# Halving three times on VectorE in the last tiles of a one-query attention

## The chip, the cores and the metric

The kernel runs on one core of one Trainium2 chip. The metric is device time in microseconds (us). A core that runs alone cannot be compared with its neighbours, so a run's state is judged from the other runs of the same kernel; all profiled runs here count as fast. Medians are given with their ranges. Ratios are computed as the mean time of one kernel's fast runs over that of the other's of the same rounds, so they are not quite the ratio of the quoted medians.

## The reference

```python
B, H, Sq, Skv, Dh = 8, 32, 1, 4096, 128          # bf16 q, k, v
scores = jnp.einsum('bhqd,bhkd->bhqk', q, k) * q.shape[-1] ** -0.5
attn = softmax(scores, axis=-1)
return jnp.einsum('bhqk,bhkd->bhqd', attn, v)
```

There are 256 heads with one query each. Every byte of K and V (537 MB together) is read once and used for one query, so the arithmetic per byte is small.

## The kernel before

Eight heads form a tile; there are 32 tiles (0 to 31), `C` = 256 rows per partition and `D` = 128. K and V tiles of 8.39 MB share three buffers. VectorE multiplies K by q in place and folds the products of each row in halves; TensorE finishes the fold by adding slices through an identity matrix into PSUM; VectorE reduces what is left to scores.

```python
LT = NT - 3                                   # tile 29
def width_of(t, lo):
    return D // 8 if lo == C // 2 and 0 < t < NT - 3 else D // 2

def product(t, lo, hi):
    part = kt[:, lo:hi, :]
    nc.vector.tensor_tensor(out=part, in0=part, in1=qb..., op=ALU.mult)
    n = D
    while n > width_of(t, lo):
        n //= 2
        nc.vector.tensor_tensor(out=part[:, :, 0:n], in0=part[:, :, 0:n],
                                in1=part[:, :, n : 2 * n], op=ALU.add)

def sum_over_d(t, lo, hi):
    ds = BANK // (hi - lo)                    # BANK = 512
    n = width_of(t, lo) // ds
    for s in range(n):
        nc.tensor.matmul(ps[:], lhsT=ident[:], rhs=kt[:, lo:hi, s * ds : (s + 1) * ds], ...)
# ... cut: scores, weights, value matmuls
# the last V tile is loaded in pieces, so that the end is short:
("v", NT - 1): [C // 2, C // 4, C // 8, C // 16, LAST // 2, LAST // 4, LAST // 4]
```

Tiles 1 to 29 are worked on in halves; the others in quarters. From tile 1 to tile 28 the second half is folded from 128 to 16 values; all other parts only from 128 to 64. A V tile is issued when the sums of the K tile whose buffer it takes are done; a K tile when the value matmuls of an older V tile are. For V tile 31 it is the value matmuls of tile 29.

Of the kernel before, what the change touches and what calls it, by code (L numbers as in the profile page):

```python
# [25 lines left out]
def kernel(  # L26
# [8 lines left out]
    B, H, Sq, D = q.shape  # L35
# [5 lines left out]
    C = S // PH  # L41
    NT = NH // G
# [85 lines left out]
    w_last = consts.tile([P, LAST, RG], BF16, name="w_last")  # L128
    nc.gpsimd.memset(w_last[:], 0.0)

    loads = {}
    loops = []

# [17 lines left out]
    def load(kind, t):  # L151
        src = k_t if kind == "k" else v_t
        buf = kv_pool.tile([P, C, D], BF16, name=f"{kind}t", tag="kv")
        c0 = 0
        for n in cuts.get((kind, t), [C]):
            dma = nc.sync.dma_start(buf[:, c0 : c0 + n, :], src[t, :, c0 : c0 + n, :])  # L156
            behind_loop(dma)
            c0 += n
            if kind == "k" and t == 0 and c0 == n:
                nc.sync.dma_start(q_all[:], q_n)  # L160
        assert c0 == C
        loads[kind, t] = buf
# [3 lines left out]
    def q_prep(t):  # L166
        x, p0 = divmod(t * G, P)
        qh = ps_q.tile([G, D], F32, name="qh", tag="qp")
        nc.tensor.matmul(  # L169
            qh[:], lhsT=ident[:, p0 : p0 + G], rhs=q_all[:, x, :], start=True, stop=True  # L170
        )
        qg = q_pool.tile([G, D], BF16, name="qg", tag="qg")
        nc.scalar.activation(out=qg[:], in_=qh[:], func=ACT.Copy)  # L173
        qp = ps_q.tile([P, D], F32, name="qp", tag="qp")
        nc.tensor.matmul(qp[:], lhsT=heads[:].rearrange("g h x -> g (h x)"), rhs=qg[:], start=True, stop=True)  # L175
        qb = q_pool.tile([P, 1, D], BF16, name="qb", tag="qb")
        nc.scalar.activation(out=qb[:, 0, :], in_=qp[:], func=ACT.Copy)  # L177
        qbs[t] = qb

    def width_of(t, lo):  # L180


        return D // 8 if lo == C // 2 and 0 < t < NT - 3 else D // 2

    def product(t, lo, hi):
        kt = loads["k", t]
        qb = qbs[t]
        part = kt[:, lo:hi, :]
        nc.vector.tensor_tensor(  # L189
            out=part, in0=part, in1=qb[:].to_broadcast([P, hi - lo, D]), op=ALU.mult  # L190
# [4 lines that stand above are left out]
            nc.vector.tensor_tensor(  # L195
                out=part[:, :, 0:n], in0=part[:, :, 0:n], in1=part[:, :, n : 2 * n], op=ALU.add
            )
# [3 lines left out]
    def sum_over_d(t, lo, hi):  # L201
        kt = loads["k", t]
        ps = ps_s.tile([P, BANK], F32, name="ps", tag="ps")
        ds = BANK // (hi - lo)
        n = width_of(t, lo) // ds
        for s in range(n):
            nc.tensor.matmul(  # L207
                ps[:], lhsT=ident[:], rhs=kt[:, lo:hi, s * ds : (s + 1) * ds],
                start=(s == 0), stop=(s == n - 1),
            )  # L210
        sums[t, lo] = ps
# [3 lines left out]
    def scores_of(t, lo, hi):  # L215
        if lo == 0:
            scs[t] = sc_pool.tile([P, C], F32, name="sc", tag="sc")
        ps = sums.pop((t, lo))[:].rearrange("p (c s) -> p c s", c=hi - lo)
        made = nc.vector.tensor_reduce(  # L219
            out=scs[t][:, lo:hi], in_=ps, axis=AX.X, op=ALU.add  # L220
        )
        if hi == C:
            behind_loop(made)
# [74 lines left out]
                one(i, start=False, stop=(i == NV - 1))  # L298
        loops.append(loop)

    LT = NT - 3

    def values_of(t, lo, hi):
        vt = loads["v", t]
        w = ws[t]
        if lo == 0:
            avs[t] = ps_v.tile([P, CB * D], F32, name="av", tag="av")
        end = C if t < NT - 1 else C - LAST


        group = [
            0 if t == NT - 1 and C // 2 <= c0 < C // 2 + 3 * C // 32 else c0 // CB % TG
            for c0 in range(0, end, CB)
        ]
        for c0 in range(lo, hi, CB):
            i = c0 // CB
            j = group[i]
            nc.tensor.matmul(  # L318
                avs[t][j * AG : (j + 1) * AG, :], lhsT=w[:, i, :, :],
                rhs=vt[:, c0 : c0 + CB, :], start=(i < TG), stop=(j not in group[i + 1 :]),  # L320
            )
# [6 lines left out]
    def norm_of(n):  # L328
        zp = ps_z.tile([RG, 1], F32, name="zp", tag="zp")
        esum = esums.pop(n)  # L330
        for r in range(R):
            nc.tensor.matmul(  # L332
                zp[:], lhsT=mine[:, r, :], rhs=esum[:, r : r + 1], start=(r == 0), stop=(r == R - 1)
            )
        zps[n] = zp
# [7 lines left out]
    def copy_of(t):  # L343
        comb = o_pool.tile([P, CB, D], BF16, name="comb", tag="comb")
        av = avs.pop(t)[:].rearrange("p (m d) -> p m d", d=D)
        n = AG if t < LT else P
        nc.scalar.activation(out=comb[0:n, :, :], in_=av[0:n, :, :], func=ACT.Copy)  # L347
        combs[t] = comb

    def result_of(t):  # L350
        n, r = divmod(t, R)
        comb = combs.pop(t)
        if r == 0:
            ops[n] = ps_o.tile([RG, D], F32, name="op", tag="op")
        e = AG if t < LT else P

        def last_rows(lo, hi):
            for i in range(lo, hi):
                nc.tensor.matmul(  # L359
                    ops[n][:], lhsT=w_last[:, i, :], rhs=loads["v", t][:, C - LAST + i, :],  # L360
                    start=False, stop=(i == LAST - 1),
                )

        if t == NT - 1:
            last_rows(0, 3 * LAST // 4)
        for m in range(CB):
            nc.tensor.matmul(  # L367
                ops[n][:], lhsT=pick[0:e, m, r, :], rhs=comb[0:e, m, :],
                start=(r == 0 and m == 0), stop=(r == R - 1 and m == CB - 1 and t < NT - 1),
            )  # L370
        if t == NT - 1:
            last_rows(3 * LAST // 4, LAST)
# [17 lines left out]
    Q, HALF = C // 4, C // 2  # L390
# [3 lines left out]
    with tc.manual_schedule(engines={E.PE, E.DVE, E.Activation, E.SP}):  # L394
        q_prep(0)
        q_prep(1)
        for t in range(NT):
            loop = 0 < t <= LT
            v_last = t >= NT - 2
            n = t // R - 1  # L400
            if not loop:
                if t + 1 < NT:
                    load("k", t + 1)
                load("v", t)
            first = HALF if loop else Q
            product(t, 0, first)
            if not loop:
                sum_over_d(t, 0, first)
            if 0 < t - 1 <= LT:
                if (t - 1) % R == 0:  # L410
                    norm_of(n)
                if t > 1:
                    result_of(t - 2)
            if t + 2 < NT:
                q_prep(t + 2)
            if loop:
                sum_over_d(t, 0, HALF)
                product(t, HALF, C)
                sum_over_d(t, HALF, C)
                scores_of(t, 0, HALF)  # L420
                if t > 2 and t % R == 1:
                    recip_of(n)
                values_loop(t - 1)
                load("k", t + 1)
                load("v", t)
                scores_of(t, HALF, C)
            else:
                product(t, Q, HALF)
                sum_over_d(t, Q, HALF)
                scores_of(t, 0, Q)  # L430
                product(t, HALF, HALF + Q)
                sum_over_d(t, HALF, HALF + Q)
                scores_of(t, Q, HALF)
                if t > 2 and t % R == 1:
                    recip_of(n)
                product(t, HALF + Q, C)
                sum_over_d(t, HALF + Q, C)
                scores_of(t, HALF, HALF + Q)
            if v_last:
                values_of(t - 1, 0, C)  # L440
            if not loop:
                scores_of(t, HALF + Q, C)
            weights_of(t)
            if t > 2 and t % R == 1:
                finish_of(n)
            if t > 0:
                copy_of(t - 1)
                if t > 2 and t % R == 1:
                    store_of(n)
                if not loop:  # L450
                    if t % R == 0:
                        norm_of(n)
                    result_of(t - 1)
        values_of(NT - 1, 0, C // 2)
        norm_of(NQ - 1)
        recip_of(NQ - 1)
        values_of(NT - 1, C // 2, C - LAST)
        copy_of(NT - 1)
        result_of(NT - 1)
        finish_of(NQ - 1)  # L460
        store_of(NQ - 1)
# [30 lines left out]
```

## Time and profile before

| | before |
|---|---|
| median (3 runs) | 1250.9 us (1250.84 to 1250.91) |
| load queue | 536.94 MB, 99.5% of 16 DMA engines' span |
| mean load rate | 430 GB/s |
| VectorE busy | 1010.6 us (81%) |
| TensorE busy | 761.4 us (61%) |

Each digit of the profile's DMA row is a fortieth of the span, and 9 is 90% or more: the row is full. The execution that was profiled took 1251.34 us, 0.4 us more than the median: it is not one of the three runs in the table.

### The profile page before, as it was taken

What the parts mean: (1) busy time and instruction counts of PE and PEld (TensorE: products, weight loads), DVE (VectorE), ACT (ScalarE), POOL (GpSimd) and SP (SyncE); (2) the same over time, 40 slices, a digit from 0 to 9 for tenths busy, and PEclk for the clock granted to TensorE, in tenths of its full rate; (3) what the DMA queues carried; (4) which work ended last, traced back from release to release, by engine and by line L of the source; (5) the groups of instructions that cost most, each with busy time, mean ns of one, the idle gap of its engine ahead of it and who ended that gap; (6) DMA issues with size and microseconds to landing.
All of it is one profiled execution on the core that took longest, in us unless ns stands there. A gap on an engine that the chain in (4) does not pass through costs nothing. (4 is left out here: it accounts for less than half of the span.)

```text
span 1249.5 us, 10534 instructions
## 1 busy us (share of the span) xinstructions
PE 761.4 (61%) x3004; PEld 284.3 (23%) x3004; DVE 1010.6 (81%) x379; ACT 166.1 (13%) x433; POOL 4.5 (0%) x24
## 2 busy tenths in 40 slices
PE   3356457554586555766557665577655676556855
PEld 1122122221222212222122222122221222212312
DVE  7877987778977789777797777987779877798694
ACT  0111011111011110111101111011110111101111
POOL 1000000000000000000000000000000000000000
PEclk9786798777887777878678777887867877778867
DMA  9999999999999999999999999999999999999998
GB/s 405 436 436 435 436 429 424 426 436 437 436 432 435 435 434 434 435 435 426 431 436 435 426 430 436 435 434 437 433 432 430 433 437 432 433 432 425 429 442 339
DMA packets 11430, 537.30 MB, mean 430 GB/s; under 512 B 1808, under 2 KB 2064, under 8 KB 2320
## 3 DMA queue, kind: packets, MB, share of 16 engines
q1 hardware_dynamic: 11072, 536.94, 99.5%
q8 instruction: 14, 0.23, 0.1%
q10 hardware_dynamic: 336, 0.07, 0.0%
q14 instruction: 8, 0.07, 0.0%
HBM read 536.94 MB, written 0.07 MB: 430 GB/s over the span
## 5 line engine op out<-in xcount | busy, mean ns | idle before, releaser
L189 DVE TENSOR_TENSOR kt<-kt,qb 128x16384 bf16<-128x16384 bf16 (+1 forms) x70 | 556.8, 7955 | 156.8 <-DMA kt<-in_k_dram 150.1
L207 PE MATMUL ps<-kt,ident 128*128 128x512 bf16 x688 | 253.2, 537 | 416.3 <-DVE kt L195 415.9
L290 PE MATMUL av<-vt,w 128*32 x1740 | 425.3, 397 | 4.4
L195 DVE TENSOR_TENSOR kt<-kt 128x4096 bf16<-128x4096 bf16 (+1 forms) x126 | 382.7, 3037 | 4.3
L290 PEld LDWEIGHTS av<-vt,w 128*32 x1740 | 173.3, 100 | 262.1 <-issue 118.9
L207 PEld LDWEIGHTS <-ident 128*128 128x128 bf16 x688 | 80.0, 125 | 583.0 <-DVE kt L195 444.7
L244 ACT ACTIVATE e<-sc,nmax 128x256 bf16<-128x256 f32 x32 | 16.2, 508 | 708.0 <-DVE nmax L238 708.0
L251 ACT ACTIVATE w<-e,mine 128x256 bf16<-128x256 bf16 x256 | 105.6, 495 | 1.1
L219 DVE TENSOR_REDUCE sc<-ps 128x128 f32<-128x512 f32 (+1 forms) x70 | 48.1, 687 | 57.0 <-PE ps L207 57.0
L347 ACT ACTIVATE comb<-av 32x512 bf16<-32x512 f32 (+1 forms) x32 | 18.8, 586 | 327.3 <-PEq L280 320.9
L276 PE MATMUL av<-vt,w 128*32 128x512 bf16 x116 | 47.1, 498 | 14.5 <-issue 13.3
L367 PE MATMUL op<-comb,pick 32*16 32x128 bf16 (+1 forms) x128 | 12.2, 213 | 21.9 <-ACT comb L347 21.9
L276 PEld LDWEIGHTS av<-vt,w 128*32 128x32 bf16 x116 | 6.9, 101 | 54.7 <-issue 54.7
L175 PE MATMUL qp<-qg,heads 8*128 8x128 bf16 x32 | 7.0, 217 | 16.7 <-ACT qg L173 16.7
L367 PEld LDWEIGHTS <-pick 32*16 32x16 bf16 (+1 forms) x128 | 8.7, 83 | 28.9 <-issue 28.5
L231 DVE TENSOR_REDUCE pmax<-sc 128x1 f32<-128x256 f32 x32 | 13.4, 420 | 1.1
L318 PE MATMUL av<-vt,w 128*32 128x512 bf16 x188 | 13.7, 417 | 0.0
L173 ACT ACTIVATE qg<-qh 8x128 bf16<-8x128 f32 x32 | 8.5, 267 | 33.5 <-PE qh L169 33.5
L169 PE MATMUL qh<-q_all,ident 128*8 128x128 bf16 x32 | 7.2, 225 | 8.7 <-DMA q_all<-in_q_dram 8.3
L177 ACT ACTIVATE qb<-qp 128x128 bf16<-128x128 f32 x32 | 8.9, 278 | 9.7 <-PE qp L175 9.7
L339 DVE RECIPROCAL rz<-zp 16x1 f32<-16x1 f32 x16 | 2.3, 147 | 8.1 <-PE zp L332 8.1
L233 DVE TENSOR_SCALAR spread<-same,pmax 128x32 f32<-128x32 f32 x32 | 7.7, 242 | 1.1
(30 smaller groups left out, 45.7 us busy)
## 6 DMA issues: line engine op xcount, KB each, us to landing
kt<-in_k_dram SPq DMA_DIRECT2D x4, 4096.0 KB, 23.8
kt<-in_k_dram SPq DMA_DIRECT2D x4, 2048.0 KB, 12.3
vt<-in_v_dram SPq DMA_DIRECT2D x1, 4096.0 KB, 33.1
vt<-in_v_dram SPq DMA_DIRECT2D x1, 2048.0 KB, 37.6
vt<-in_v_dram SPq DMA_DIRECT2D x1, 1024.0 KB, 39.7
vt<-in_v_dram SPq DMA_DIRECT2D x1, 512.0 KB, 40.5
vt<-in_v_dram SPq DMA_DIRECT2D x31, 26.2
kt<-in_k_dram SPq DMA_DIRECT2D x29, 28.7
```

The costliest lines, as they stand in the source:

```text
L189: nc.vector.tensor_tensor(out=part, in0=part, in1=qb[:].to_broadcast([P, hi - lo, D]), op=ALU.mult)
L195: nc.vector.tensor_tensor(out=part[:, :, 0:n], in0=part[:, :, 0:n], in1=part[:, :, n : 2 * n], op=ALU.add)
L207: nc.tensor.matmul(ps[:], lhsT=ident[:], rhs=kt[:, lo:hi, s * ds : (s + 1) * ds], start=(s == 0), stop=(s == n - 1),)
L219: made = nc.vector.tensor_reduce(out=scs[t][:, lo:hi], in_=ps, axis=AX.X, op=ALU.add)
L231: nc.vector.tensor_reduce(out=pmax[:], in_=sc[:], axis=AX.X, op=ALU.max)
L244: nc.scalar.activation(out=e[:], in_=sc[:], func=ACT.Exp, bias=nmax[:, 0:1], scale=scale, accum_out=esums[t // R][:, t % R : t % R + 1],)
L251: nc.scalar.activation(out=w[:, :, g, :], in_=e_g, func=ACT.Copy, scale=mine[:, 0, g : g + 1])
L276: pe.matmul(av, lhsT=wf[:, i * nw : (i + 1) * nw], rhs=vf[:, i * nv : (i + 1) * nv], **how)
L290: pe.matmul(av, lhsT=wf[:, bass.ds(ow + i * nw, nw)], rhs=vf[:, bass.ds(ov + i * nv, nv)], start=False, stop=False,)
L318: nc.tensor.matmul(avs[t][j * AG : (j + 1) * AG, :], lhsT=w[:, i, :, :], rhs=vt[:, c0 : c0 + CB, :], start=(i < TG), stop=(j not in group[ ...
L347: nc.scalar.activation(out=comb[0:n, :, :], in_=av[0:n, :, :], func=ACT.Copy)
L367: nc.tensor.matmul(ops[n][:], lhsT=pick[0:e, m, r, :], rhs=comb[0:e, m, :], start=(r == 0 and m == 0), stop=(r == R - 1 and m == CB - 1 an ...
```

## The change

The intent: in three places near the end, TensorE needs 16 or 8 identity matmuls to finish a sum, at half clock, while VectorE waits. Folding these parts further on VectorE leaves 4 or 2 matmuls, so that the buffers come free and the weights are ready earlier.

```diff
     def width_of(t, lo):
-        return D // 8 if lo == C // 2 and 0 < t < NT - 3 else D // 2
+        if t == 0:
+            return D // 2
+        return D // 8 if lo == (C // 2 if t <= LT else 3 * C // 4) else D // 2
```

The rest of the diff moves `LT` up and renames `loop` to `halves`. So tile 29's second half and the last quarters of tiles 30 and 31 are now folded to 16 values.

More of the change, by code (lines that the diff above doesn't have):

```diff
@@ L129 @@
     nc.gpsimd.memset(w_last[:], 0.0)
+    LT = NT - 3
     loads = {}
@@ L299, in values_loop @@
         loops.append(loop)
-    LT = NT - 3
     def values_of(t, lo, hi):
@@ L397 @@
         for t in range(NT):
-            loop = 0 < t <= LT
+            halves = 0 < t <= LT
             v_last = t >= NT - 2
             n = t // R - 1
-            if not loop:
+            if not halves:
                 if t + 1 < NT:
@@ L404 @@
                 load("v", t)
-            first = HALF if loop else Q
+            first = HALF if halves else Q
             product(t, 0, first)
-            if not loop:
+            if not halves:
                 sum_over_d(t, 0, first)
@@ L415 @@
                 q_prep(t + 2)
-            if loop:
+            if halves:
                 sum_over_d(t, 0, HALF)
@@ L440 @@
                 values_of(t - 1, 0, C)
-            if not loop:
+            if not halves:
                 scores_of(t, HALF + Q, C)
@@ L449 @@
                     store_of(n)
-                if not loop:
+                if not halves:
                     if t % R == 0:
```

## The prediction

> **What bounds the kernel now.** I read the page first: its busy slices, its queue table, and its costliest groups.
>
> ```profile
> PE 761.4 (61%) x3004; PEld 284.3 (23%) x3004; DVE 1010.6 (81%) x379; ACT 166.1 (13%) x433; POOL 4.5 (0%) x24
> ...
> DMA  9999999999999999999999999999999999999998
> GB/s 405 436 436 435 436 429 424 426 436 437 436 432 435 435 434 434 435 435 426 431 436 435 426 430 436 435 434 437 433 432 430 433 437 432 433 432 425 429 442 339
> ...
> q1 hardware_dynamic: 11072, 536.94, 99.5%
> ...
> L189 DVE TENSOR_TENSOR kt<-kt,qb 128x16384 bf16<-128x16384 bf16 (+1 forms) x70 | 556.8, 7955 | 156.8 <-DMA kt<-in_k_dram 150.1
> L207 PE MATMUL ps<-kt,ident 128*128 128x512 bf16 x688 | 253.2, 537 | 416.3 <-DVE kt L195 415.9
> ```
>
> The DMA row shows no free slice, and the load queue is busy for 99.5% of the span. VectorE (DVE) is busy for 81% and spends 150.1 us waiting for K to land; TensorE (PE) waits 416 us for VectorE. So everything computes faster than data arrives. Each K or V tile is 128 x 256 x 128 bf16 = 8.39 MB, which at the page's mean of 430 GB/s takes 19.5 us; 64 tiles take 1,249 us of a 1,249.5 us span.
>
> A bound that holds on average may still break at the end, where the change sits, so I read the chain of waits that ended last.
>
> ```profile
> 1196.02 3.40 PE ps L207 x8
> 1199.41 3.60 PE av L318 x64
> 1203.01 0.02 issue
> 1203.03 0.33 SPq L156
> ...
> 1204.83 40.66 DMA vt<-in_v_dram
> 1245.48 0.04 issue
> 1245.53 0.83 PE op L359 x12
> 1246.36 0.22 PE op L367 x4
> 1246.58 0.24 PE op L359 x4
> ```
>
> The tempting reading is that the eight matmuls at 1196.02, which the change cuts to two, gate the issue of the last V tile and hence the end. But 40.66 us from issue to landing is twice what a tile needs at 430 GB/s: the transfer stood in a queue. V tile 30 was issued at 1199.45 and tile 31 from 1203.03, and those two alone need 39.0 us (2 x 19.5). Counting back from 1246 they start flowing at about 1207, so the rest of K tile 31 still occupied the queue for some 7 us after 1199.45. The stretches confirm it:
>
> ```profile
> 1180.00:1200.00 20.00, 10.97 (x46) 3.69 (x48) 15.68 (x8) 0.00 (x0) 0.00 (x0) 0.74 0.97 414
> 1200.00:1227.00 27.00, 14.25 (x88) 4.86 (x80) 26.76 (x15) 4.39 (x11) 0.00 (x0) 0.61 1.00 431
> 1227.00:1240.00 13.00, 8.29 (x91) 3.51 (x95) 4.17 (x6) 4.63 (x12) 0.76 (x4) 0.76 0.98 418
> 1240.00:1246.20 6.20, 6.07 (x69) 3.25 (x59) 0.16 (x1) 0.60 (x1) 0.00 (x0) 0.72 0.67 258
> ```
>
> The last three columns are TensorE's clock, the DMA share and GB/s. DMA is full up to 1240 and falls only while the small last pieces of V drain.
>
> **What the Trainium skill says.** "DMA: Bandwidth & Descriptors", section "Where 436 GB/s comes from", derives a ceiling of 435.2 GB/s from the 16 memory ports; the slices here reach 432 to 437, so it agrees and no room is left in the rate. "VectorE: DVE Perf Modes", section "Side-by-side: where the cycles go for N=2048 bf16", counts half a cycle per element in the two-per-cycle mode plus about 158 cycles at 0.96 GHz: 1224 ns for 2048 elements; the trace has 1225. "TensorE: Matmul & The Clock Gate", part 1, says that the array runs at half clock until it has been busy for about 3.4 us (512 columns then start every 427 ns instead of 216) and falls back after an idle window; the trace agrees, with a granted clock of 0.50 or 1.00 and eight matmuls of 512 columns in 3.60 us at 0.50.
>
> **The change part by part.** Halving from 64 to 16 values per row adds two VectorE adds and divides the identity matmuls of that part by four.
>
> Tile 29, second half: it adds one add of 4096 elements (2.29 us in the groups by shape, but 2.21 from start to start because the ends overlap) and one of 2048 (1.23 busy, 1.14 start to start): 3.35 us. It takes 16 matmuls down to 4. The sixteen took 6.47 us here; four took 1.89 us for tile 28, which already has this form. Saved 4.58, net 4.58 - 3.35 = **1.2 us** earlier for this tile's scores, for the issue of V tile 29 (now 1162.25), and for the loop of value matmuls behind it, which takes 16.7 us on tiles 27 and 28 alike.
>
> Tiles 30 and 31, last quarter: one add of 2048 elements (1.14) and one of 1024. No 1024-element add exists in this trace; the steps 4425, 2292, 1225 ns halve their distance each time and give 0.69 us, and the skill's count gives (512 + 158)/0.96 GHz = 0.70, an estimate; some 0.60 start to start. So 1.74 us are added. Eight matmuls become two: two at half clock are estimated at 1.05 us (0.63 for one, as its longest record, plus 0.43). Tile 30's eight took 3.40 and tile 31's 3.60, so 0.6 and 0.8 us are gained.
>
> Sum of the path: 1.2 + 0.6 + 0.8 = **2.6 us** earlier for the weights of tile 31, which ScalarE now finishes at 1238.39 (1235.09 + 3.30). V tile 30's issue moves from 1199.45 to about 1197.6, V tile 31's to about 1201.5. All of this only makes queue entries older: the same bytes still leave at the same rate, and the 40.66 us of the last wait become about 42. VectorE work rises by 3.5 + 2 x 1.9 = 7.4 us to about 1018, inside its idle time. TensorE loses 12 + 6 + 6 = 24 matmuls.
>
> The end then. Here is TensorE's work from the last weights on:
>
> ```profile
> 1239.39 2.96 PE L318 MATMUL av<-vt,w 128*32 128x512 bf16 x29
> 1242.14 0.29 PE L332 MATMUL zp<-esum,mine 128*16 128x1 f32 x4
> 1242.30 3.09 PE L318 MATMUL av<-vt,w 128*32 128x512 bf16 x28
> 1245.53 0.83 PE L359 MATMUL op<-vt,w_last 128*16 128x128 bf16 x12
> 1246.19 0.39 PE L367 MATMUL op<-comb,pick 128*16 128x128 bf16 x4
> 1246.42 0.39 PE L359 MATMUL op<-vt,w_last 128*16 128x128 bf16 x4
> ```
>
> The first half of V tile 31 lands at 1236.2 (issued at 1203.03, 33.1 us to landing), the 2 MB piece at about 1241.1, the 1 MB piece at about 1243.6, the 512 KB piece at about 1244.9 and the last 128 KB at 1246.2 (issued at 1226.5, 19.7 us). Four matmuls of the 28 read the 512 KB piece, so these 28, whose last one ends at 1245.39, are already at the heels of the data. The weights being 2.6 us earlier moves the first 32 value matmuls from 1239.2 to about 1236.5, but the last 28 cannot end before 1245.2, the copy of 0.60 us and the closing matmuls follow as now, and the last 128 KB is needed anyway. I put the gain of the whole change at **0 to 0.3 us**.
>
> **The rivals.** (a) *The chain is taken at its word*: V tile 31 is issued 1.5 us earlier and so ends earlier, for 1249.4. For it: the chain does run through these matmuls. Against: the full DMA row and the 40.66 us. It would hold only if the queue ran dry near 1200. (b) *A colder TensorE at the end*: with the weights earlier, TensorE finishes the first half by 1238 to 1240 and then idles until 1241.1. Today it works without a gap from 1239.2, and the clock is 0.55 in 1241.1 to 1243.7 and 1.00 after. If the gap delays the return of the full clock, the first six of the 28 matmuls, which add into one place one after another, cost 6 x 0.43 = 2.6 us (to 1243.7), and the other 22, four at a time, 0.107 each = 2.4 us (to 1246.1 instead of 1245.0). That is 1.1 us later, up to 1.5 with the closing matmuls: 1252.0 to 1252.4. Against: a stretch two thirds busy may count as busy. I give it one chance in three. (c) *VectorE becomes the bound*: 7.4 us more work where it has nearly no gap (26.76 of 27 us in 1200 to 1227). Against: each add replaces a longer wait for matmuls, and V does not need VectorE; had all 7.4 us come on top, the weights would be ready at 1245.8 and the end some 7 us later, 1258. One chance in fifty.
>
> **Range and chances.** No change two times in three (1250.6 to 1251.1, as the runs agree within 0.1 us), 1 to 1.5 us slower nearly one time in three, a fraction of a microsecond to 1.5 faster otherwise. The weighted middle is 1251.0, range 1250.0 to 1252.4. Two per cent is 25 us; the work that the change touches lies in the last 95 us, all under a full DMA queue, so faster or slower by that has one chance in a hundred each.
>
> **What would show it.** Right: VectorE about 1018 us and x385, TensorE x2980, the last 512-column sums of tiles 30 and 31 x2, V tile 30 issued near 1197.6, the last V wait lengthened to about 42 us, weights of tile 31 near 1235.8, the last V landing within 0.5 us of 1246.2. Wrong: a DMA share visibly below 0.97 between 1180 and 1227, V landing earlier by as much as it was issued earlier, or a last landing moved by over 1 us. Rival (b) shows as a granted clock of 0.50 after 1243.7 with the copy of the last values later than 1246. What could spoil the whole estimate is a load rate that reacts to VectorE's changed timing; nothing in the slices hints at it.

## The result, and the profile after

| | before | after |
|---|---|---|
| median | 1250.9 us (1250.77 to 1251.86, 6 runs) | 1251.45 us (1251.4 to 1251.59, 6 runs) |
| ratio | | 1.0004, 95% interval 0.9991 to 1.0016 |

The change makes no difference worth the name. Yet there is a small pattern. Five of the six runs before lie at 1250.77 to 1250.91, the sixth at 1251.86, and all six after at 1251.4 or more. The computed interval includes 1 all the same. We come back to this half microsecond below.

The page of the changed kernel:

```profile
PE 759.8 (61%) x2980; PEld 282.2 (23%) x2980; DVE 1017.9 (81%) x385; ACT 166.1 (13%) x433; POOL 4.4 (0%) x24
...
DMA  9999999999999999999999999999999999999997
...
q1 hardware_dynamic: 11072, 536.94, 99.5%
```

The work changed exactly as counted (VectorE six instructions and 7.3 us more, TensorE 24 matmuls fewer) and the load queue looks as before. The chain of waits that ended last:

```profile
1194.52 1.24 DVE kt L197
...
1195.78 0.70 DVE kt L197
...
1196.53 1.03 PE ps L209 x2
1197.56 6.03 PE av L318 x47
...
1203.61 0.33 SPq L157
...
1205.41 40.28 DMA vt<-in_v_dram
...
1245.74 0.83 PE op L359 x12
```

The two new adds (1.24 and 0.70 us) and the pair of matmuls in 1.03 us are there. V tile 30 is issued at 1197.60 instead of 1199.45. But the issue of V tile 31 moved from 1203.03 to 1203.61: in this execution it is **later**. The 64 value matmuls of tile 29 before it took 6.07 us instead of 3.64, because TensorE got its full clock late: 1197.5 to 1203.6 shows a mean clock of 0.59 here and 0.87 before. This differs from one execution to the next. In a second trace of the same kernel (run change_again below) the clock was 0.76 there, the 64 matmuls took 5.10 us, and V tile 31 was issued at 1202.59, earlier than before. And 1205.41 + 40.28 is still 1245.7: neither the earlier nor the later issue shows in the landing.

TensorE from the last weights on, and the stretches around it (the third last column is the clock):

```profile
1236.97 1.89 PE L318 MATMUL av<-vt,w 128*32 128x512 bf16 x29
1238.69 0.24 PE L332 MATMUL zp<-esum,mine 128*16 128x1 f32 x4
1241.37 1.89 PE L318 MATMUL av<-vt,w 128*32 128x512 bf16 x16 [2.44 <-DMA vt<-in_v_dram]
1243.84 0.62 PE L318 MATMUL av<-vt,w 128*32 128x512 bf16 x8 [0.58 <-DMA vt<-in_v_dram]
1245.09 0.40 PE L318 MATMUL av<-vt,w 128*32 128x512 bf16 x4 [0.63 <-DMA vt<-in_v_dram]
1245.74 0.83 PE L359 MATMUL op<-vt,w_last 128*16 128x128 bf16 x12 [0.25 <-DMA vt<-in_v_dram]
```

```profile
1239.20:1241.10 1.90, 0.00 (x0) 0.00 (x0) 0.00 (x0) 0.00 (x0) 0.00 (x0) 1.00 0.97 394
1241.10:1243.70 2.60, 1.89 (x16) 0.78 (x16) 0.00 (x0) 0.00 (x0) 0.00 (x0) 1.00 0.79 310
1243.70:1244.90 1.20, 0.62 (x8) 0.21 (x8) 0.00 (x0) 0.00 (x0) 0.00 (x0) 1.00 0.43 161
```

The brackets show where the gain went: every group of value matmuls after the first now waits for its piece of V (2.44, 0.58, 0.63, 0.25 us). In the kernel before, the same matmuls ran without such waits, just behind the data. The 2.4 us gained in the weights (1235.97 instead of 1238.39) became waiting for DMA.

### The profile page after: what moved, and what is told of

It reads as the page before. It is cut to its first block, busy times and chain, and to the rows that moved or that the text cites. A ratio compares the mean times of both kernels' runs of the same rounds, so it can differ in the third digit from the quotient of the medians.

```text
span 1249.7 us, 10492 instructions
## 1 busy us (share of the span) xinstructions
PE 759.8 (61%) x2980; PEld 282.2 (23%) x2980; DVE 1017.9 (81%) x385; ACT 166.1 (13%) x433; POOL 4.4 (0%) x24
## 5 line engine op out<-in xcount | busy, mean ns | idle before, releaser
L209 PE MATMUL ps<-kt,ident 128*128 128x512 bf16 x664 | 248.6, 543 | 417.9 <-DVE kt L197 417.5
L197 DVE TENSOR_TENSOR kt<-kt 128x8192 bf16<-128x8192 bf16 (+2 forms) x132 | 390.0, 2955 | 4.5
L209 PEld LDWEIGHTS <-ident 128*128 128x128 bf16 x664 | 77.3, 125 | 582.0 <-DVE kt L197 446.0
L278 PE MATMUL av<-vt,w 128*32 128x512 bf16 x116 | 47.5, 503 | 14.7 <-issue 13.3
L318 PE MATMUL av<-vt,w 128*32 128x512 bf16 x188 | 16.1, 480 | 3.6 <-DMA vt<-in_v_dram 3.6
L233 DVE TENSOR_REDUCE pmax<-sc 128x1 f32<-128x256 f32 x32 | 13.4, 420 | 1.1
L318 PEld LDWEIGHTS <-w 128*32 128x32 bf16 x188 | 6.6, 117 | 13.3 <-issue 11.0
## 6 DMA issues: line engine op xcount, KB each, us to landing
kt<-in_k_dram SPq DMA_DIRECT2D x4, 2048.0 KB, 12.9
```

The costliest lines, as they stand in the source:

```text
L233: nc.vector.tensor_reduce(out=pmax[:], in_=sc[:], axis=AX.X, op=ALU.max)
L278: pe.matmul(av, lhsT=wf[:, i * nw : (i + 1) * nw], rhs=vf[:, i * nv : (i + 1) * nv], **how)
L318: nc.tensor.matmul(avs[t][j * AG : (j + 1) * AG, :], lhsT=w[:, i, :, :], rhs=vt[:, c0 : c0 + CB, :], start=(i < TG), stop=(j not in group[ ...
```

## The experiments

The diffs are excerpts: lines that only create a tile or pass a value on are cut.

Two theories about the main question. **Full queue**: the end is set by the last byte, and an earlier issue only makes a queue entry older. **Chain**: the end follows the issue of the last V tile, and the change gained little because its parts cancel. A third, **instruction fetch**, came from comparing the traces, for the half microsecond. The profile lists the DMA engines' fetches of instructions as queues of their own (packets, MB, share). In 1150 to 1246 us, the second of these queues has, in the kernel before,

```profile
q14 instruction: 1, 0.01, 0.0%
```

and in the changed one

```profile
q14 instruction: 2, 0.02, 0.0%
```

The additional fetch lies at 1214 to 1218 us; in the kernel before, the fetch like it comes after the last instruction. Counting VectorE's instructions with its waits (447 before, 453 after), its earlier fetches fall where 60, 190 or 191, and 316 had begun, about every 128; the next is due near 444. Six more instructions bring that point from the end of the program into the loading. (It came when 436 had begun in the change and 434 in the quarters alone, below. That it is VectorE's fetch is inferred from this count alone, and the count gives the place only roughly.) The Trainium skill, "Runtime: NRT & Kernel Launch", section "Instruction fetch mechanics", says that each sequencer fetches its next block of instructions by its own DMA queue, at a mostly hidden cost; and "DMA: Bandwidth & Descriptors", section "Queues, rings and completion order", that each DMA engine takes turns between its queues. So a fetch would take time from one of the 16 engines, and each load here has 16 landings in the trace, one for each engine.

### The change again

The same kernel on the chip that ran the next three.

> The change itself once more, on one chip with its parts. Full-queue theory: the load queue is busy to the end, so the time is that of the kernel before, within noise (1250.9, ratio 1.000). Instruction-fetch theory: VectorE's program is six instructions longer, so its next fetch of instructions falls into the loading instead of after it and holds up one of the 16 DMA engines: 1251.4 to 1251.5, a ratio of 1.0004 or 1.0005 with an interval that leaves 1 out.

Measured: 1251.46 us (1251.34 to 1251.66, 5 runs) against 1250.87 (1250.73 to 1251.66, 9 runs), ratio 1.0004 (0.999 to 1.0017). The pattern repeats at the same size, though the computed interval again does not leave 1 out, as I had expected it to. One of the nine runs before, at 1251.66, is as slow as the change. The trace of this run also bears on rival (b) of the prediction, a colder TensorE:

```profile
1241.42 4.19 PE L318 MATMUL av<-vt,w 128*32 128x512 bf16 x28 [2.54 <-DMA vt<-in_v_dram]
```

```profile
1241.10:1243.70 2.60, 2.27 (x14) 0.83 (x14) 0.00 (x0) 0.00 (x0) 0.00 (x0) 0.56 0.78 309
```

After a gap of 2.54 us the clock did fall here, to a mean of 0.56, where the first trace of the change has 1.00 after 2.44 us. The 28 matmuls ended at 1245.61 instead of 1245.49, and the closing matmuls began at 1245.76 instead of 1245.74.

### Six idle instructions in the kernel before

```diff
+        if (t == NT - 3 and lo == C // 2) or (t > NT - 3 and lo == 3 * C // 4):
+            for _ in range(2):
+                nc.vector.tensor_copy(out=pad[:, 1:2], in_=pad[:, 0:1])
```

> The kernel before with six one-element VectorE copies put where the change has its six adds; matmuls, sums and issue times as before. Instruction-fetch theory: 1251.4, as the change, with one more fetch on the second instruction queue before 1246 us. Chain theory and full-queue theory alone (the time follows from the work or from the data): 1250.9, no difference to the kernel before.

Measured: 1251.49 us (1251.39 to 1251.57, 5 runs). Folds and matmuls are those of the kernel before, and the time is that of the change, with two fetches on the second instruction queue in the window. The rate in the last stretch, 1240 to 1246 us in 40 slices, shows what it does. Kernel before:

```profile
GB/s 191 300 410 328 437 437 437 396 410 369 423 321 437 396 430 338 362 314 261 217 297 239 348 212 239 219 178 164 178 171 177 178 178 171 184 178 116 41 0 0
```

The change:

```profile
GB/s 345 562 336 498 273 454 328 492 335 492 335 498 341 396 280 287 246 260 287 205 266 232 239 218 164 164 184 184 178 157 143 157 130 246 62 27 20 27 20 7
```

The kernel before with six idle copies:

```profile
GB/s 546 382 546 259 521 217 480 335 422 386 464 386 382 457 239 321 123 294 218 212 259 212 239 259 205 157 205 191 218 178 184 191 198 178 75 27 20 27 20 7
```

In both kernels with the additional fetch, the loading ends with a thin tail of 20 to 27 GB/s. One sixteenth of 435 GB/s is 27: a single engine is probably still at work. Before, several engines end together at 116 and 41.

### The change with six instructions fewer

```diff
+        if n < 6:                 # six reciprocals left out: wrong for 96 heads, on purpose
+            zps.pop(n); rzs[n] = ones; return
```

> The change with six reciprocals of earlier tiles left out (wrong results for 96 heads on purpose), so that VectorE has as many instructions as before. Instruction-fetch theory: 1250.9, the fetch is back after the end of the loading. Rival, the later issue of V tile 31 (1203.6 instead of 1203.0 us) or its warmer tail costs the 0.5 us: stays at 1251.4.

Measured: 1251.04 us (1250.71 to 1251.45, 5 runs), one fetch in the window. The median falls by 0.4 us, as the fetch theory says, but the runs spread more than elsewhere and one is as slow as the change. By itself this run would settle nothing.

### The parts alone

```diff
+        return D // 8 if lo == C // 2 and t <= LT else D // 2          # tile 29 alone
```

> Only the second half of tile 29 is halved three times. Full-queue theory: 1250.9, with V tile 29 issued near 1160.9 instead of 1162.25. Instruction-fetch theory: two instructions more bring the fetch to about 1235 to 1243 us, so between 1250.9 and 1251.4. If the two parts of the change had cancelled each other, this one would show over 1 us either way.

Measured: 1250.92 us (1250.89 to 1251.12, 5 runs), V tile 29 issued at 1160.81, one fetch in the window. The place of the next fetch was a miss: I expected it at 1235 to 1243 us, and it came at 1249.53, after the last load.

```diff
+        return D // 8 if lo == (C // 2 if t < LT else 3 * C // 4) and t != LT else D // 2   # quarters alone
```

> Only the last quarters of tiles 30 and 31 are halved three times. Full-queue theory: the time of the kernel before within 0.5 us. Instruction-fetch theory: four instructions more, the fetch at some 1220 to 1235 us, 1251.4. If the parts had cancelled, over 1 us either way.

Measured: 1251.41 us (1251.29 to 1251.56, 5 runs), two fetches in the window. So neither part does anything large, and the parts do not cancel. The medians split by fetch, not by fold. The trace's landing records give each engine's end of the last V piece, counted from the first load packet:

```text
                    second fetch   second last engine   last engine   this execution   median
before                  no              1244.26           1244.31       1251.34        1250.9
tile 29 alone           no              1243.70           1243.74       1250.92        1250.92
change minus six        no              1243.74           1243.84       1250.95        1251.04
quarters alone          yes             1243.93           1244.50       1251.41        1251.41
change                  yes             1243.85           1244.54       1251.45        1251.45
before plus six         yes             1243.84           1244.53       1251.44        1251.49
```

With the fetch the last engine trails by 0.57 to 0.69 us, without it by 0.04 to 0.10 (and by 0.22 in the next experiment). The fetch's own packet took 0.33 us, so it accounts for about half of the lag; the rest stays open. So does the first row: the profiled execution of the kernel before was as slow as the change without a second fetch and without a trailing engine, its last engines ending together, 0.57 us later than with tile 29 alone. The fetch is thus one way to lose half a microsecond here, not the only one.

### V issued far earlier

```diff
+        if t == NT - 2 and lo >= C // 2:
+            return                     # tile 30's last two quarters not multiplied: wrong on purpose
```

> The kernel before with tile 30's last two quarters not multiplied and halved at all (wrong on purpose): some 13 us of VectorE work less ahead of the issue of V tiles 30 and 31, which are then issued near 1188 and 1191 instead of 1199.5 and 1203. Chain theory: the end moves by the same 10 to 13 us, 1238 to 1241. Full-queue theory: 1250.9 within 0.6 us, the wait of the last V piece grows from 40.7 to about 52 us.

Measured: 1251.16 us (1250.86 to 1251.23, 4 runs), ratio 1.0002 (0.9986 to 1.0017). V tile 30 was issued at 1186.59, 12.9 us earlier, and the last wait in the chain grew from 40.66 to 48.03 us (I expected 52; V tile 31 gained less than tile 30):

```profile
1197.08 48.03 DMA vt<-in_v_dram
```

The wait ended at 1245.11 instead of 1245.48, and the time did not fall. The chain theory, which expected 1238 to 1241, is refuted.

### V issued later

```diff
+        if t == NT - 2 and lo in (3 * C // 4,): product_once(t, lo, hi)   # tile 30: again
+        if t == NT - 1 and lo in (3 * C // 4,): return                    # tile 31: not at all
```

> Tile 30's last quarter is multiplied and halved twice over, tile 31's not at all (wrong on purpose): V tiles 30 and 31 are issued 6.7 us later, near 1206.1 and 1209.7, while tile 31's weights come at the same time as before. Chain theory: 1257.6. Full-queue theory: K tile 31 occupies the queue until about 1206 to 1207, and a new transfer takes about 2 us to flow, so the queue stands empty for 1 to 2 us: 1252 to 1253.

Measured: 1253.49 us (1253.2 to 1254.44, 4 runs), ratio 1.002 (1.0005 to 1.0035). The second run does the same with two quarters:

```diff
-        if t == NT - 2 and lo in (3 * C // 4,): product_once(t, lo, hi)
-        if t == NT - 1 and lo in (3 * C // 4,): return
+        if t == NT - 2 and lo in (C // 2, 3 * C // 4): product_once(t, lo, hi)
+        if t == NT - 1 and lo in (C // 2, 3 * C // 4): return
```

> The same with two quarters: V tiles 30 and 31 are issued 13.3 us later, near 1212.8 and 1216.4. Chain theory: 1264.2. Full-queue theory: the queue stands empty from about 1206.5 to 1214.5, some 8 us: 1258.5 to 1259.5, with a DMA share that falls visibly in this stretch.

Measured: 1260.77 us (1259.72 to 1261.24, 4 runs), ratio 1.0076 (1.0061 to 1.0092). Its stretches, with the DMA share and GB/s as the last two columns:

```profile
1200.00:1206.00 6.00, 0.00 (x0) 0.00 (x0) 5.93 (x3) 0.00 (x0) 0.00 (x0) 0.68 0.61 262
1206.00:1210.00 4.00, 0.39 (x1) 0.13 (x2) 3.96 (x3) 0.00 (x0) 0.00 (x0) 0.50 0.00 0
1210.00:1216.00 6.00, 6.00 (x68) 2.51 (x70) 3.16 (x6) 1.32 (x4) 0.00 (x0) 0.80 0.53 175
```

The queue ran dry: 0 GB/s in 1206 to 1210. V tile 30 was issued 6.4 us late (1205.83) for 2.6 us of loss, and 13.4 us late (1212.88) for 9.9. The difference, **3.8 and 3.5 us**, is what the queue held in reserve. It is a rough figure, since the issues are of one execution each and the losses of medians: with the profiled executions' own times (1254.44 and 1261.24 against 1251.34 us) it is 3.3 and 3.5, and V tile 30's issue alone was at 1198.33 in the kernel with idle copies, which computes the same. The runs came out 0.5 and 1.3 us above the upper ends of the full-queue estimates, because I had counted the reserve as about 5 us: DMA already falls to a share of 0.61 in 1200 to 1206. The 16 engines do not finish together (in the kernel before, their landings of one load lie 3.3 us apart at 1207.0), and the first packet of V tile 30 started 0.96 us after its issue. The full queue was right, but it is not deep.

### Fewer bytes

```diff
+        for n in [C // 2] if (kind, t) == ("k", 15) else cuts.get((kind, t), [C]):
```

The second half of K tile 15 is neither loaded nor used; the first half is worked on twice.

> Only half of K tile 15 is loaded; its second half is computed over the first half again (wrong on purpose), so all engines work as before. Full-queue theory: 4.19 MB less at 430 GB/s, 9.75 us less: 1241.2. If compute were the bound anywhere, less than that.

Measured: 1250.27 us (1248.98 to 1251.4, 4 runs), ratio 0.9998 (0.9982 to 1.0013). This is a miss. (The wrong half still passes the comparison, which is therefore loose here.) The stretches of the profiled run say why:

```profile
570.00:580.00 10.00, 2.27 (x5) 0.55 (x6) 8.52 (x6) 0.00 (x0) 0.00 (x0) 0.50 0.41 177
...
610.00:620.00 10.00, 1.82 (x4) 0.42 (x4) 8.68 (x6) 0.00 (x0) 0.00 (x0) 0.50 0.82 354
```

After the shorter load the queue ran dry, because the next one was not issued until its buffer came free. At the 433 GB/s of 80 to 1140 us in the kernel before, these two stretches lost 5.9 and 1.8 us, 7.7 of the 9.75 saved; the profiled run was 1.9 us faster. Why two other runs gained nothing stays open.

### Much more folding

```diff
+        return D // 8 if t <= LT or lo == 3 * C // 4 else D // 2
```

> The change, and the first half of tiles 1 to 29 halved three times as well: 58 more VectorE adds, 3.35 us more of VectorE per tile (about 1115 us in all, 89%), 348 matmuls fewer. Full-queue theory: still within 1 us of 1250.9, for each tile's VectorE work of some 33 to 34 us stays under the 38.7 us that its data takes. Instruction-fetch theory: one VectorE fetch more as in the change, but some three TensorE fetches fewer, so 1249.5 to 1251.5. VectorE-bound theory: 10 us or more slower.

Measured: 1271.08 us (1269.49 to 1271.46, 5 runs), ratio 1.0159 (1.0145 to 1.0173): my largest miss. VectorE is still only 88% busy and still waits 68 us for K. Two lines of VectorE's timeline, with the DMA queue's own issue of V, in the kernel before:

```profile
547.71 8.69 DVE L189 TENSOR_TENSOR kt<-kt,qb 128x16384 bf16<-128x16384 bf16 x1 [5.34 <-DMA kt<-in_k_dram]
...
579.49 0.33 SPq L156 DMA_DIRECT2D vt<-in_v_dram  x1
```

and in this kernel:

```profile
554.28 8.69 DVE L191 TENSOR_TENSOR kt<-kt,qb 128x16384 bf16<-128x16384 bf16 x1 [1.94 <-DMA kt<-in_k_dram]
...
589.63 0.33 SPq L157 DMA_DIRECT2D vt<-in_v_dram  x1
```

From the landing of K to the next issue it takes 31.8 us before and 35.4 here: 3.6 us more, about what the queue held in reserve at the end. V issues then follow each other every 39.4 us (510.89 to 589.63 is two tiles) instead of 38.8 (501.78 to 734.31 is six); 29 tiles of 0.61 us are 18 of the 20 us lost. The prediction named a rival for such a loss, a load rate that reacts to VectorE's changed work. The trace's packet records settle it: between 100 and 1100 us the loads ran at 384 GB/s in the 6 us after each V issue, but at 432 after each K issue and 433 in the rest, where the kernel before has 432, 432 and 433. So the load slows down only where V is issued late. VectorE need not be busy all the time to set the pace: landing, folding, issue and landing again form a loop. The DMA row does not show it: it is 9 in all slices but the last here too, and the load queue's share is 99.0%. The rate does, 423 GB/s over the span instead of 430.

The body of the value loop was shortened on top of this:

```diff
-LOOP = 6
+LOOP = 3
```

> The same with three instead of six matmuls in the body of the value loop, so some 170 TensorE instructions fewer to fetch. Instruction-fetch theory: a fetch fewer than the run before, 1249 to 1251. If the loop's overhead grows over some 5 us per tile, K is issued later, but still under a full queue: no loss up to about 5 us.

Measured: 1304.63 us (1297.5 to 1308.2, 5 runs), ratio 1.0423 (1.0396 to 1.045). The longest wait of a K issue for the value loop grew from 16.6 to 22.3 us; it lies in the same loop. In the packet records the loads now fall to 337 GB/s in the 6 us after a K issue, against 418 after a V issue and 430 in the rest, so it is K that is issued late. How exactly 5.7 us become 1.2 us per tile I did not work out.

The last run folds everything to 16 values:

```diff
+        return D // 8
```

> Every part of every tile halved three times. Full-queue theory: as the two before, 1249.5 to 1251.5; the last weights some 2 us earlier than with the change, for nothing. VectorE-bound theory: slower by 10 us or more.

Measured: 1278.53 us (1277.03 to 1280.27, 5 runs), ratio 1.0218 (1.0204 to 1.0232), 7.5 us worse still. The few TensorE fetches saved are nothing beside this. No version that does all the work beats the kernel before.

## Why the prediction was right

- **"The change gains nothing because the queue is full"**: right. V tile 30 was issued 1.85 us earlier in the change and 12.9 us earlier in the experiment, and the end stayed. This was tested, not only argued.
- **The path sum, 2.6 us**: the weights of tile 31 came at 1235.97 instead of 1238.39, 2.4 us earlier. The terms hold too: V tile 29's issue moved by 1.4 us (1.2 said), V tile 30's to 1197.60 (1197.6 said). That these two fit so closely is partly luck: in the kernel with six idle copies, which folds tile 29 as before, V tile 29 was issued at 1160.90, as early as in the change (1160.86), since its 16 matmuls took 5.50 us instead of 6.47. A pair of matmuls took 1.03 us (1.05 estimated) and the 1024-element add 0.70 us (0.69 or 0.70 estimated; the count of 158 cycles behind the second gives 1231 ns for 2048 elements, where the page prints 1224 and the trace has 1225).
- **"V tile 31's to about 1201.5" and the last wait of 42 us**: wrong (and its own terms, 1.2 + 0.6 us earlier, give 1201.2). It went to 1203.61 and 40.28, and to 1202.59 and 41.33 in the second trace of the change. I took the 64 value matmuls of tile 29 as fixed at 3.60 us; at a clock not yet full they took 6.07 and 5.10 us. It cost nothing, for the same reason that the gain brought nothing.
- **"0 to 0.3 us" for the end**: the value matmuls were piece-bound, as said. The measured difference is +0.5 us, from something that was not in the sum. The median of 1251.45 lies outside the 1250.6 to 1251.1 given for no change. It lies inside the whole range of 1250.0 to 1252.4 because that was widened for rival (b), whose cost did not come: that part is luck.
- **Rival (b), a colder TensorE**: its clock came in one of two traces of the change, its cost in neither. In the first the clock was 1.00 through the gap of 2.44 us and to the end; in the second it was 0.56 in 1241.1 to 1243.7 after a gap of 2.54 us, yet the run took the same time, 1251.46 us. The sum of 1.1 to 1.5 us went wrong where it kept all 28 matmuls at half clock: they took 4.19 us, not 5.0, and the clock was back at 1.00 in 1244.9 to 1246.2. The page cited in the prediction ("TensorE: Matmul & The Clock Gate", part 1) asks for an idle window of about 3.4 us before the clock falls; the second trace does not agree, as the gap in which it fell was shorter. The kernel before, too, had a clock of 0.55 in 1241.1 to 1243.7, after a wait of 2.65 us.
- **Rival (c), VectorE as the bound**: right to reject for 7.4 us spread over three tiles that shorten a longer wait; but its reason, "so everything computes faster than data arrives", is too comfortable, and so is reading it from a full DMA row. The reserve is about 3.5 us, and 3.4 us of folding in every tile cost 20 us under a row of nines.
- **The half microsecond**: not foreseen. Five rows of the table, with the idle copies as the cleanest, support that VectorE's next instruction fetch moved into the loading and held up one DMA engine; the first row fits neither way. It is shown that six idle instructions suffice and that the medians split by that fetch. That the delay passes through exactly that engine is read from the landing records and not shown, and the kernels without it have single runs as slow (1251.34, 1251.45, 1251.66 and 1251.86 us).

## What to carry to other kernels

When a DMA queue is full, shortening the chain that issues into it changes only how long its entries wait; test it by moving the issue both ways, which also measures, roughly, how much reserve the queue has. A full DMA row alone does not show that there is reserve: kernels 20 and 54 us slower had it too. A busy share of 81% is not a reserve of 19%: follow the loop from landing through work to the next issue, and compare it with the time of the data. For effects under a microsecond count instructions as well as work, since a fetch of instructions is a DMA too, and take a second trace of the same kernel before reading a cause from clock or issue times.

## What the Trainium skill lacked or had wrong

- "Runtime: NRT & Kernel Launch", "Instruction fetch mechanics", calls the cost of crossing a block mostly hidden. For a load-bound kernel it lacks that a fetch seems to hold up one of the 16 DMA engines: medians of 1251.41 to 1251.49 us with one more fetch in the loading against 1250.87 to 1251.16 without. After the first fetch of the kernel before (16 KB, at 97.6 us) the spread of the engines' landings of one load went from 0.3 us (landed at 81.3) to 1.6 (landed at 101.9).
- The same section gives 16 KiB blocks. The fetches on one instruction queue are of that size (14 of 0.23 MB in all); those on the other are of about 8 KB (8 of 0.07 MB), and VectorE's come about every 128 instructions.
- "DMA: Bandwidth & Descriptors", "Where 436 GB/s comes from", has about 358 GB/s bind for loads from HBM. One core alone read at 430 GB/s over the whole span. (The page's own measurement with the pair's other core idle, 425 GB/s for 16 MB, is near that; the sentence lacks this condition.)
- No page says how much earlier than the end of the running load the next one must be issued. Here V tile 30 could be some 3.5 us later than in the kernel before, where K tile 31 had an estimated 7 us still to flow.
